# Banded attention and a gated feed-forward: moving the attention steps in the output part, and turning the fourth x tile by DMA

## The chip, the cores and the metric

The kernel runs on one core of a Trainium2 chip. The time is microseconds (us) of device time. Runs of one kernel agree within about half a percent. "Span" is the time from the first to the last instruction in a trace; it is some 2 us shorter than the time of the run. A run counts as fast when it is within 1.5% of the fastest run of its kernel.

## The reference

Attention over 8 batches, 8 heads, 576 tokens, 64 per head, with a band of 32 tokens to either side and 8 global tokens; its result x (4608 tokens by 512) goes through a gated feed-forward.

```python
mask = np.abs(pos[:, None] - pos[None, :]) <= window
mask = mask | is_global[:, None] | is_global[None, :]
scores = np.where(mask, scale * np.matmul(q, k.transpose(0, 1, 3, 2)), -1000000000.0)
attn = softmax(scores)                     # written out in the reference
x = np.matmul(attn, v)                     # then heads side by side: (4608, 512)
ffn_out = gelu(x @ w_gate) * (x @ w_val) @ w_out
out = x + sigmoid(x @ w_res) * ffn_out
```

## The kernel before

Nine chunks of 512 tokens (four tiles of 128). For chunk c an input part makes twelve pairs of products g and v (`g_ps`, `v_ps`), then an output part of 16 steps makes, for each tile t, a gate product (`r_ps`) and three thirds of the output product (`f_ps`). Between these 16 steps stands the attention of chunk c + 1: scores (`sc`), exponentials (`pt`), global rows (`sn`, `vgs`), values (`nd`), the normalised tile (`xtok`), and its turned form (`xt`, its transpose), which the next input part multiplies. A turn is made either by TensorE (four transposes and a copy) or by one DMA, issued on the sync queue. The products are written to banks of PSUM, which the pools `psm` and `pss` hand out; a bank is free again when its reader is done. The reader of a gate product is the tanh on ScalarE, from which the sigmoid is made; the readers of scores are the exponentials. Chunks 1 to 7 have this form; chunk 0 has its own.

```python
psm = ctx.enter_context(tc.tile_pool(name="psm", bufs=4, space=bass.MemoryType.PSUM))
pss = ctx.enter_context(tc.tile_pool(name="pss", bufs=2, space=bass.MemoryType.PSUM))

def scores(c, quad, pps=(0, 1)):
    ...
    for pp in pps:
        pool, tag = (psm, "mm") if pp else (pss, "sc")
        sc = [pool.tile([128, 2, 4, 64], F32, name="sc", tag=tag) for _ in range(2)]
        heads(c, quad, pp, sc, True)
        ...

def turn_x(c, t):
    mine = xt[c % 2][:, :, 128 * t:128 * t + 128]
    if c > 1 and t < 3:
        nc.sync.dma_start(mine, xtok[c % 2][:, t, :], transpose=True)
        return
    tx = pss.tile([128, NKT, 128], BF16, name="tx", tag="sc")
    for kk in range(NKT):
        nc.tensor.transpose(tx[:, kk, :], xtok[c % 2][:, t, 128 * kk:128 * kk + 128], ident)
    (nc.vector.tensor_copy if c or t == 3 else nc.scalar.copy)(mine, tx)

# the end of a tile's third third: the output goes through GpSimd and the sync queue
    nc.vector.scalar_tensor_tensor(prb, held["r"], 1.0, held["f"], ALU.add, ALU.mult)
    nc.gpsimd.tensor_tensor(ob, prb, xtok[c % 2][:, t, :], ALU.add)
    nc.sync.dma_start(out[r0:r0 + 128, :], ob)

# the 16 steps; jobs[n] stand before product n
    jobs[1] += [lambda: half(0), lambda: held_mask[0](0, 4)]
    for t in range(4):
        jobs[5 + 2 * t].append(lambda t=t: values(c + 1, t))
        jobs[7 + 2 * t].insert(0, lambda t=t: turn_x(c + 1, t))
    jobs[4].append(lambda: half(1))
    ...
```

The softmax here doesn't subtract the row's maximum and nothing guards it: scores larger than these inputs give would overflow.

## Time and profile before

The median was 393.49 us of three runs.

| what | before |
|---|---|
| TensorE busy, share of the span | 377.8 us, 97% |
| VectorE, ScalarE, GpSimd | 51%, 43%, 43% |
| share of the last chain on TensorE | 93% |
| output part, chunks 1, 3, 5 | 18.68 us |
| output part, chunks 2, 4, 6 (one tile has two batches) | 18.89 to 18.90 us |
| output part, chunk 7 (no global rows) | 19.06 us |
| first g of chunk 1 (end of the start-up) | 70.35 us |

An output part is measured from the start of its first r product to the start of the next chunk's first g product, both read from TensorE's row.

### The profile page before, as it was taken

How to read it: one execution, taken by the hardware profiler on the slowest of the kernel's cores; microseconds unless marked ns; L12 is line 12 of the kernel's file. 1: busy time of each engine (PE TensorE's matmuls, PEld its weight loads, DVE VectorE, ACT ScalarE, POOL GpSimd, SP SyncE). 2: the span in 40 equal slices, each digit the busy share in tenths (PEclk: the TensorE clock that was granted, in tenths of full speed). 3: DMA queues.
4: the chain of work that ended last, by engine and by line, in shares of the span. 5: the costliest groups of instructions: out<-in, count | busy, mean ns of one | idle time of the engine just before them, and what ended most of it. 6: DMA issues, size and time to landing. Idle time of an engine off the chain costs nothing.

```text
span 391.4 us, 8491 instructions
## 1 busy us (share of the span) xinstructions
PE 377.8 (97%) x3360; PEld 196.8 (50%) x3360; DVE 201.2 (51%) x446; ACT 170.2 (43%) x285; POOL 168.2 (43%) x203
## 2 busy tenths in 40 slices
PE   3989989999999999999999999999999999999996
PEld 2674555444644464445544554455445544554444
DVE  7767684537534664467344643555345533553422
ACT  6753685236243633364335423462337233723321
POOL 7787783958165425562456138612501210121012
PEclk9999999999999999999999999999999999999999
DMA  8999999699659924996399729992990210041002
GB/s 249 258 379 357 239 349 210 129 189 155 105 99 162 169 51 108 133 192 75 106 143 183 79 82 144 199 91 81 118 146 30 72 51 0 2 94 57 0 28 81
DMA packets 153002, 52.78 MB, mean 135 GB/s; under 512 B 136386, under 2 KB 143426, under 8 KB 152962
## 3 DMA queue, kind: packets, MB, share of 16 engines
q1 hardware_dynamic: 77024, 41.88, 44.7%
q0 software_dynamic: 75392, 9.84, 42.9%
q8 instruction: 26, 0.43, 0.5%
q10 hardware_dynamic: 546, 0.52, 0.4%
q14 instruction: 14, 0.11, 0.1%
HBM read 39.19 MB, written 9.44 MB: 124 GB/s over the span
## 4 chain that ended last, share of the span: by engine, by line
PE 93%; DVE 3%; ACT 2%; DMA 1%; issue 1%; SPq 0%; POOL 0%; DVEq 0%; POOLq 0%; ACTq 0%
PE g_ps L630 24%; PE v_ps L630 23%; PE f_ps L686 22%; PE r_ps L656 8%; PE nd L575 5%; PE sc L534 2%; PE nd L587 2%; PE ss L481 1%; PE sg L472 1%; PE tx L610 1%; DMA xt<-xtok 1%; PE sc L523 1%; PE tk L451 1%; PE tq L451 1%; ACT pt L541 1%
## 5 line engine op out<-in xcount | busy, mean ns | idle before, releaser
L639 DVE SCALAR_TENSOR_TENSOR ht<-gsb,v_ps 128x512 bf16<-128x512 bf16 x108 | 74.2, 687 | 97.0 <-PE v_ps L630 91.4
L636 ACT ACTIVATE gsb<-g_ps 128x512 bf16<-128x512 f32 x108 | 64.4, 597 | 124.5 <-PE g_ps L630 124.4
L692 POOL TENSOR_TENSOR ob<-prb,xtok 128x512 f32<-128x512 f32 x35 | 40.2, 1153 | 174.0 <-DVE prb L690 174.0
L630 PE MATMUL g_ps<-xt,wg_t 128*128 128x512 bf16 (+1 forms) x456 | 112.0, 368 | 0.4 <-DMA xt<-xtok 0.4
L630 PE MATMUL v_ps<-xt,wv_t 128*128 128x512 bf16 (+1 forms) x456 | 112.0, 368 | 0.0
L686 PE MATMUL f_ps<-wo_t,ht 128*128 128x512 bf16 x420 | 99.0, 379 | 0.0
L630 PEld LDWEIGHTS <-wg_t 128*128 128x128 bf16 x456 | 43.3, 98 | 49.4 <-issue 0.9
L630 PEld LDWEIGHTS <-wv_t 128*128 128x128 bf16 x456 | 43.4, 98 | 49.1
L686 PEld LDWEIGHTS <-ht 128*128 128x128 bf16 x420 | 40.0, 98 | 39.5
L664 ACT ACTIVATE rsb<-r_ps 128x512 bf16<-128x512 f32 x36 | 21.8, 609 | 67.0 <-PE r_ps L656 67.0
L690 DVE SCALAR_TENSOR_TENSOR prb<-rsb,f_ps 128x512 f32<-128x512 bf16 x35 | 24.0, 686 | 27.2 <-PE f_ps L686 26.3
L656 PE MATMUL r_ps<-wr_t,xt 128*128 128x512 bf16 x144 | 36.9, 380 | 1.1 <-ACT rsb L664 1.0
L541 ACT ACTIVATE pt<-sc 128x512 bf16<-128x512 f32 x64 | 33.2, 620 | 9.5 <-PE sc L534 9.5
L91 POOL DMA_DIRECT2D q_st<-in_q_dram x25 | 21.5, 869 | 19.0 <-DMA qt<-q_st 18.6
L575 PEld LDWEIGHTS <-pt 128*128 128x128 bf16 x576 | 21.9, 97 | 9.3 <-PE r_ps L656 0.7
L557 DVE TENSOR_TENSOR pt<-pt,maskw 128x512 bf16<-128x512 bf16 x56 | 22.4, 421 | 7.1 <-ACT pt L541 5.8
L99 POOL DMA_DIRECT2D ve<-in_v_dram x30 | 25.5, 865 | 0.0
L600 DVE TENSOR_TENSOR xtok<-nd,rden 128x512 bf16<-128x512 f32 x34 | 23.5, 692 | 1.3
L91 POOL DMA_DIRECT2D k_st<-in_k_dram x25 | 21.1, 878 | 4.2 <-DMA kt<-k_st 2.6
L575 PE MATMUL nd<-ve,pt 128*128 128x65 bf16 x320 | 22.4, 193 | 0.6 <-DVE xtok L600 0.6
L599 DVE RECIPROCAL rden<-nd 128x8 f32<-128x8 f32 x34 | 7.0, 207 | 30.3 <-PE nd L587 30.3
L656 PEld LDWEIGHTS <-xt 128*128 128x128 bf16 x144 | 13.0, 97 | 14.8 <-issue 0.9
(174 smaller groups left out, 305.6 us busy)
## 6 DMA issues: line engine op xcount, KB each, us to landing
out_dram<-ob SPq DMA_DIRECT2D x35, 256.0 KB, 2.1
vo<-ve SPq DMA_DIRECT2D x12, 260.0 KB, 5.3
q_st<-in_q_dram POOLq DMA_DIRECT2D x20, 128.0 KB, 5.4
k_st<-in_k_dram POOLq DMA_DIRECT2D x20, 128.0 KB, 6.4
ve<-in_v_dram POOLq DMA_DIRECT2D x18, 128.0 KB, 6.2
wo_t<-in_k_dram SPq DMA_DIRECT2D x8, 256.0 KB, 5.4
vraw<-in_q_dram SPq DMA_DIRECT2D x8, 256.0 KB, 6.8
extra<-in_moe_w_out_dram SPq DMA_DIRECT2D x4, 512.0 KB, 6.7
```

The lines of the kernel that those rows point to most:

```text
L91: nc.gpsimd.dma_start(dst[0:n, r, :].rearrange("p (h d) -> p h d", d=D), src[b].rearrange("h s d -> s h d")[128 * r:128 * r + n])
L99: nc.gpsimd.dma_start(t[p0:p1, c, :, 0:D], v[b].rearrange("h s d -> s h d")[s0 + p0:s0 + p1])
L541: nc.scalar.activation(sc if stay else mine, sc, ACTF.Exp, bias=0.0, scale=SCALE)
L575: nc.tensor.matmul(nds[h // 4][:, VG * (h % 4):VG * (h % 4) + VG], view(pt, 0, 128, c0, [[1, 128]]), vw, start=(h % 4 == 0 and e == 0), st ...
L600: nc.vector.tensor_tensor(xtok[c % 2][:, t, :].rearrange("p (a h d) -> p a h d", a=2, d=D), num[:, :, :, 0:D], view(rden, 0, 128, 0, [[4, ...
L630: nc.tensor.matmul(held[what][:, c0:c1], w[:, kk, 128 * j:128 * j + 128], x[:, kk, c0:c1], start=(kk == 0), stop=(kk == NKT - 1))
L636: nc.scalar.activation(held["s"], held["g"], ACTF.Gelu, bias=0.0, scale=1.0)
L639: nc.vector.scalar_tensor_tensor(ht[:, j, :], held["s"], 0.5, held["v"], ALU.mult, ALU.mult)
L656: nc.tensor.matmul(r_ps, xt[c % 2][:, kk, 128 * t:128 * t + 128], wr_t[:, kk, :], start=(kk == 0), stop=(kk == NKT - 1))
L686: nc.tensor.matmul(held["f"], ht[:, j, 128 * t:128 * t + 128], wo_t[:, j, :], start=(j == 0), stop=(j == NFF - 1))
L690: nc.vector.scalar_tensor_tensor(prb, held["r"], 1.0, held["f"], ALU.add, ALU.mult)
L692: nc.gpsimd.tensor_tensor(ob, prb, xtok[c % 2][:, t, :], ALU.add)
```

## The change

The intent was to take the last TensorE turn out of the output parts and to give the DMA turn that replaces it the time that it needs. The attention steps move about one step earlier: global rows and second scores to step 3, values to steps 4, 6, 8 and 10, each with its turn right behind. The tanh of tile 0 moves behind the first exponentials.

```diff
-        if c > 1 and t < 3:
+        if c > 1:
             nc.sync.dma_start(mine, xtok[c % 2][:, t, :], transpose=True)
...
-        if c == 0:
+        if c == 0 or t == 0:
             gates.append((gate, open_gate))
...
-                jobs[4].append(lambda: global_rows(b))
+                jobs[3].append(lambda: global_rows(b))
...
-            jobs[1] += [lambda: half(0), lambda: held_mask[0](0, 4)]
+            jobs[1] += [lambda: half(0), gates[-1][1], lambda: held_mask[0](0, 4)]
+            jobs[3].append(lambda: half(1))
             for t in range(4):
-                jobs[5 + 2 * t].append(lambda t=t: values(c + 1, t))
-                jobs[7 + 2 * t].insert(0, lambda t=t: turn_x(c + 1, t))
-            jobs[4].append(lambda: half(1))
-            jobs[6].append(lambda: held_mask[1](0, 2))
-            jobs[7].append(lambda: held_mask[1](2, 4))
+                jobs[4 + 2 * t] += [lambda t=t: values(c + 1, t), lambda t=t: turn_x(c + 1, t)]
+            jobs[5].append(lambda: held_mask[1](0, 2))
+            jobs[6].append(lambda: held_mask[1](2, 4))
...
-            work_f[n]()
+            if n == 0 and c + 1 < NCH:
+                gates[-1][0](now=False)
+            else:
+                work_f[n]()
```

## The prediction

> **What bounds the kernel now.** I read the page's busy times first, then the chain of work that ended last, then that chain inside one of the repeated stages, then the waits of every engine there. The kernel handles nine chunks of 512 tokens. Each of chunks 1 to 7 is a feed-forward input part (twelve pairs of g and v products) followed by an output part of 16 steps (per token tile t one gate product r, then three thirds of f), and the attention of the next chunk is woven into those 16 steps. The change touches only these seven output parts.
>
> ```profile
> PE 377.8 (97%) x3360; PEld 196.8 (50%) x3360; DVE 201.2 (51%) x446; ACT 170.2 (43%) x285; POOL 168.2 (43%) x203
> PE   3989989999999999999999999999999999999996
> PEclk9999999999999999999999999999999999999999
> PE 93%; DVE 3%; ACT 2%; DMA 1%; issue 1%; SPq 0%; POOL 0%; DVEq 0%; POOLq 0%; ACTq 0%
> ```
>
> TensorE is busy in nearly every slice from the second to the last but one, at full granted clock, and 93% of the chain that ended last is TensorE. The other engines stand near half. So a microsecond is won only by giving TensorE less to do or by closing a gap in its row. The chain through one output part (chunk 2, attention of chunk 3) shows how few gaps there are. Columns: start in us, length in us, what.
>
> ```profile
> 132.66 0.88 PE r_ps L656 x4
> 133.54 0.57 PE sc L534 x32
> 134.12 2.70 PE f_ps L686 x12
> 136.81 0.17 PE sn L507 x4
> 136.99 0.28 PE sn L510 x20
> 137.27 0.57 PE sc L534 x32
> 137.84 0.97 PE r_ps L656 x4
> ...
> 147.04 0.86 PE f_ps L686 x4
> 147.90 0.86 PE r_ps L656 x4
> 148.77 0.22 PE tx L610 x4
> 148.99 2.59 PE f_ps L686 x12
> 151.58 0.86 PE g_ps L630 x4
> ```
>
> Each row starts where the one before ended: no wait of TensorE in 18.92 us (132.66 to 151.58). Twelve f products take 2.59 us, 0.216 each; four r products 0.86. The only excess is 0.11 us on the f or r row behind each block of scores (2.70, 0.97). The table of waits for TensorE is empty in the output parts of chunks 1 to 6. In chunk 7 it is not:
>
> ```profile
> 353.32 1.02 PE L630 MATMUL g_ps<-xt,wg_t 128*128 128x512 bf16 x4 [0.39 <-DMA xt<-xtok]
> ```
>
> Here the first g product of chunk 8 waited for an x tile turned by DMA. On the sync engine's row the second and third of that chunk's three turns are one merged entry, and the longer part of it is the second alone:
>
> ```profile
> 347.46 4.18 SPq L606 DMA_TRANSPOSE xt<-xtok  x2
> ```
>
> In the earlier chunks the same pair took 2.52 us. So one issue took 2.86 us in place of 1.2, and the third turn came 1.6 us late.
>
> **What the Trainium skill says.** "TensorE: Matmul & The Clock Gate", section "Part 4: PE-mode transpose", gives about 275 ns for a 128x128 transpose in a kernel's context. This trace has 219 ns as the mean of one, but four of them advance the chain by only 0.22 us, because they overlap. The page "Trainium Kernel Development and Optimization", section "Performance Expectations", warns of just this: matmul busy time is a bad metric, since matmuls are pipelined. I use the 0.22. "DMA: Bandwidth & Descriptors", section "Rules for kernel authors", advises to issue a DMA early and wait for its semaphore late, so that the fixed cost overlaps; the trace agrees, as the x turns take a median of 2.4 us from issue to landing and six of seven chunks never wait for one. "Runtime: NRT & Kernel Launch", section "Instruction fetch mechanics", says that each engine fetches its program through its own DMA queue in blocks of 16 KiB. The page lists 26 such packets of 0.43 MB together, one of them in the 8 us around the slow issue above; that it caused the slowness is a guess.
>
> **The change, part by part.** The built program's order confirms what the diff says.
>
> Removed: in seven chunks the TensorE turn of tile 3 (four transposes with their weight loads, 28 in all) and its VectorE copy (425 ns, seven of them). Read from the table of groups, 28 x 219 ns would be 6.1 us; read from the chain it is 7 x 0.22 = 1.55 us. The copy lies on a half-idle engine: nothing.
>
> Added: seven DMA turns on the sync queue, about 1.2 us of issue each and 2.4 to 2.7 us to landing. This queue is idle for most of the output part.
>
> Moved on TensorE: the products themselves are the same. A block of scores is followed by f in both places now, so the two excesses of 0.11 us stay. The tile chains: values at steps 4, 6, 8, 10 in place of 5, 7, 9, 11. Between values 1, 2 and 3 still stand 1.73 us of products (two f thirds, or one f third and one gate), which the normalisation on VectorE must fit into: from the end of values 1 to the end of its masks took 1.64 us in chunk 2 (142.17 to 143.81). It fits by 0.09 us, as before, and the masked half that comes last is read some 0.24 us later.
>
> The new last turn: values 3 end at X. The normalised tile is ready at about X + 0.97 (147.04 to 148.01 before). The third turn is issued by about X + 0.6, so the fourth starts at X + 1.0 and lands at X + 3.4 to 3.7. The next g product comes at X + 1.73 (two f thirds) + 0.86 (gate) + 2.59 (three thirds) = X + 5.18. Slack 1.4 us or more. Hidden, in the rule.
>
> The gate of tile 0: its tanh now stands behind the first four exponentials. Exponentials start 0.45 us behind their scores and follow at 0.49 us. With r at 0, scores start at 0.88, exponentials run 1.33 to 3.3, tanh ends near 3.9. The next scores take the PSUM bank of that gate in their second half, at 0.88 + 0.57 + 1.84 (eight f) + 0.45 (sn) + 0.29 = 4.03. It fits by about 0.1 us. In chunk 7 there are no global rows (no sn), so the same point comes at 3.58 and TensorE waits some 0.35 us. Against that, in the kernel before, a similar wait in chunk 7 cost about 0.1 us.
>
> The end of chunk 7: before, g starts 0.55 us later than the sequence of products alone would have it (353.32 against 352.77). With tiles 0 to 2 issued earlier and the fourth with 1.4 us of slack I expect this to go.
>
> Sum: 6 x 0.22 = 1.33; chunk 7: 0.22 + 0.55 + 0.1 - 0.35 = 0.52. Together 1.85 us. I keep back 0.15 for the two fits of 0.1 us. 393.49 - 1.7 = 391.8.
>
> **Rivals.** First: the fourth DMA turn becomes the wait. If one issue is slow by 1.6 us (as at 347.46) and it is the third or fourth turn of a chunk, landing comes at X + 5.0 to 5.3, against X + 5.0 for the first weight load of g: up to 0.3 us per case, more if landing is slow too. The program of TensorE is shorter by 8 instructions a chunk, so block fetches fall elsewhere. Even one such case in each of seven chunks is some 2 us, which makes the time 393.6. For it speaks the chunk 7 wait; against it that five of six other chunks show no issue over 1.25 us and none shows a wait. Second: ScalarE's late tanh or the masks hold the second scores or values 2 in every chunk. Each fit is 0.1 us; were I wrong by 0.3 us in both, 7 x 0.4 = 2.8 us of loss would give about 394.5. Against it: both relations are worked out from the same trace's pitches, and the masks' relation is unchanged. Third: the moved work closes hidden bubbles, and more than the turns is won. Speaking against it: the chain has no gap in chunks 1 to 6, so beyond 2 us there is nothing to win in these stages; 391.0 at best.
>
> **Range and chances.** The three runs of before spread over 1.1 us, so a median may be off by half a microsecond. With the rivals, 390.9 to 393.4 should hold it 8 times in 10. The 2% limit is 7.9 us away: faster by 2% would need more than five times the removed work, slower by 2% over 1.3 us of new wait in every chunk. Within 2%: 0.98; faster 0.01; slower 0.01.
>
> **What will show it.** Right, if the chain through chunk 2's output part has no transposes and lasts about 18.7 us, if TensorE's waits stay empty in chunks 1 to 6, if the first g product of chunk 8 has no DMA wait any more, and if the scores of chunk 7 wait 0.3 to 0.4 us for the tanh. Wrong, if g products show waits for x tiles in several chunks, if the second scores wait for the tanh in chunks 1 to 6, or if the time per chunk fell by clearly more than 0.22 us.

## The result, and the profile after

The changed kernel took 391.89 us (median of six, 391.42 to 392.42) against 393.51. The ratio is 0.995, with a 95% interval of 0.9929 to 0.9971: within 2%, as forecast. A ratio here is the mean time of one kernel's fast runs over that of the other's of the same rounds, so it is not quite the ratio of the medians.

The page of the changed kernel shows the same picture as before, a little shorter:

```profile
PE 372.5 (96%) x3281; PEld 195.5 (50%) x3332; DVE 200.7 (52%) x439; ACT 171.6 (44%) x285; POOL 169.0 (43%) x203
PE   3989989999999999999999999999999999999996
```

TensorE still bounds it. Its busy time cannot be compared with before to a microsecond, because the trace holds 3281 of its products and 3332 of their weight loads: some records of products are missing. Positions in time are safe. The second trace of the changed kernel holds all 3332 of both: TensorE is busy for 376.3 us there, 1.5 us less than before.

The chain through the output part of chunk 2 in the changed kernel (start, length, what):

```profile
134.61 1.83 PE f_ps L686 x8
136.45 0.17 PE sn L507 x4
...
146.45 0.22 PE nd L587 x2
146.68 0.05 issue
146.73 1.67 PE f_ps L686 x7
148.40 0.86 PE r_ps L656 x4
149.27 2.59 PE f_ps L686 x12
151.86 0.86 PE g_ps L630 x4
```

The `tx` row is gone, and g follows f at once. The small "issue" row stands where a record is missing (seven f products are listed of eight): rows still start where those before them end. The output part lasts 18.68 us in place of 18.90.

| output part of chunk | 1 | 2 | 3 | 4 | 5 | 6 | 7 |
|---|---|---|---|---|---|---|---|
| before, us | 18.68 | 18.90 | 18.68 | 18.89 | 18.68 | 18.90 | 19.06 |
| after, us | 18.45 | 18.68 | 18.46 | 18.67 | 18.46 | 18.67 | 18.01 |

Six chunks gain 1.34 us together and chunk 7 gains 1.05: 2.39 us. The spans differ by only 1.7 us (391.4 and 389.7), because the changed kernel came to chunk 1 later in this trace, at 71.07 us in place of 70.35. Input parts and the tail after the first g of chunk 8 are alike to 0.04 us.

Chunk 7 is where the reading was too coarse. This is the chain of the kernel before at the head of that output part:

```profile
335.33 0.60 ACT rsb L664
335.93 0.02 issue
335.94 1.28 ACT L541
337.23 0.01 issue
337.24 2.07 ACT pt L541 x4
339.31 0.04 issue
339.35 1.02 PE r_ps L656 x4
```

The tanh stands first, then the load of the exponential table (1.28 us), then four exponentials, and only their end releases the second gate product. In the changed kernel the table load comes ahead of the tanh, while TensorE still works on the gate, and the same place is on TensorE throughout:

```profile
334.67 0.57 PE sc L534 x32
...
337.08 0.57 PE sc L534 x32
337.65 0.97 PE f_ps L686 x4
```

### The profile page after: what moved, and what is told of

Same layout as the page of the kernel before. It is cut to its first block, busy times and chain, and to the rows that moved or that the text cites. A ratio compares the mean times of both kernels' runs of the same rounds, so it can differ in the third digit from the quotient of the medians.

```text
span 389.7 us, 8394 instructions
## 1 busy us (share of the span) xinstructions
PE 372.5 (96%) x3281; PEld 195.5 (50%) x3332; DVE 200.7 (52%) x439; ACT 171.6 (44%) x285; POOL 169.0 (43%) x203
## 4 chain that ended last, share of the span: by engine, by line
PE 90%; DVE 3%; DMA 2%; issue 1%; ACT 1%; POOL 1%; SPq 0%; DVEq 0%; POOLq 0%
PE g_ps L630 24%; PE v_ps L630 23%; PE f_ps L686 22%; PE r_ps L656 7%; PE nd L575 4%; PE sc L534 3%; PE nd L587 2%; DMA extra<-in_k_dram 2%; PE ss L481 1%; PE sg L472 1%; DVE pt L557 1%; PE sc L523 1%; PE tk L451 1%; PE tq L451 1%; PE sn L510 1%
## 5 line engine op out<-in xcount | busy, mean ns | idle before, releaser
L686 PE MATMUL f_ps<-wo_t,ht 128*128 128x512 bf16 x398 | 96.7, 379 | 1.8 <-issue 1.0
L656 PE MATMUL r_ps<-wr_t,xt 128*128 128x512 bf16 x134 | 35.6, 378 | 1.3 <-ACT rsb L664 0.9
L557 DVE TENSOR_TENSOR pt<-pt,maskw 128x512 bf16<-128x512 bf16 x56 | 24.7, 461 | 4.1 <-ACT pt L541 2.8
L575 PE MATMUL nd<-vo,pt 128*128 128x65 bf16 x256 | 19.7, 193 | 0.4 <-PE r_ps L656 0.3
```

The source lines that it names most:

```text
L557: nc.vector.tensor_tensor(m, x, view(maskw, 0, 128, 64 * i0, [[0, 2], [64, 4], [1, 64]]), ALU.mult)
L575: nc.tensor.matmul(nds[h // 4][:, VG * (h % 4):VG * (h % 4) + VG], view(pt, 0, 128, c0, [[1, 128]]), vw, start=(h % 4 == 0 and e == 0), st ...
L656: nc.tensor.matmul(r_ps, xt[c % 2][:, kk, 128 * t:128 * t + 128], wr_t[:, kk, :], start=(kk == 0), stop=(kk == NKT - 1))
L686: nc.tensor.matmul(held["f"], ht[:, j, 128 * t:128 * t + 128], wo_t[:, j, :], start=(j == 0), stop=(j == NFF - 1))
```

## The experiments

Nine kernels ran, all with correct results. Seven were timed in rounds beside the kernel before.

### The changed kernel again

No edit.

> The changed kernel again, with five rounds. Theory A: the output parts lose 2.4 us in all (six times 0.22 and 1.06 in chunk 7, as in the first profiles), and the 0.72 us by which the changed kernel reached chunk 1 later in its first profile (71.07 against 70.35) is the spread of the start-up, which the change does not touch; then the median should be 1.6 to 2.4 us below before (ratio 0.994 to 0.996), and the first g of chunk 1 in this profile may fall anywhere from 70 to 71.5. Rival B: the later start-up belongs to the change; then the first g of chunk 1 is again near 71.1 and the ratio stays at 0.9957 or above.

Measured: 391.10 us against 393.66, ratio 0.9941 (0.9927 to 0.9954). The output parts were the same to 0.01 us, 18.01 in chunk 7 again. The first g of chunk 1 stood at 70.76 us. Over the traces with an unchanged start-up (these two, the kernel before twice, and the experiments on the output parts below) it moved between 70.35 and 71.59 us, with the kernel before at 70.35 and 71.06. The later start belongs to the spread of the start-up and not to the change. Rival B falls.

### The kernel before again

No edit, a single look.

> The kernel before again, for one more look at the start-up and at which DMA turn is issued slowly. Theory A: the first g of chunk 1 moves by some tenths of a microsecond from 70.35, output parts of chunks 1 to 6 last 18.68 and 18.90 us again. Chunk 7 loses about 0.3 us to the exponentials in every run (that is in the order of the program), while the 0.55 us at its end appear only if a block of program is fetched during the second or third turn again.

Measured: 393.44 us, span 391.7. The output parts were as before but for two. Chunk 5 took 18.88 in place of 18.68. The list of waits names nothing, but the semaphore events in the trace do: of the sixteen parts in which the third turn reports its landing, fifteen were in by 272.13 us and the last came at 273.74, while a 16 KiB block of program had been fetched from 271.57 to 272.55. The weight load of the next g had to wait for it (0.50 us idle, 0.12 in the first trace), and g began 0.20 us late:

```profile
273.84 0.56 PEld L630 LDWEIGHTS <-wg_t 128*128 128x128 bf16 x4 [0.50 <-issue]
```

So a turn can also land late although it was issued in the usual 1.2 us. Chunk 7 took 18.54 us in place of 19.06, and no wait is listed before its first g, although its second turn was issued slowly again (2.18 us). So of the 0.83 us that chunk 7 lost in the first trace, some 0.3 belong to the order of the program and 0.5 to the chance that a slow issue is slow enough.

### The fourth turn by DMA, in the old order

```diff
 # the kernel before
-        if c > 1 and t < 3:
+        if c > 1:
```

> The old order of steps with tile 3 turned by DMA too, nothing else. Theory A: in the old order the fourth turn stands on the sync queue behind the output of tile 2, whose data are ready only about 2.9 us after values 3 end; issued there, it lands about 1.5 us after the next chunk's first g could start, so each of seven chunks gains 0.22 and loses about 1.6: 9 to 10 us slower than before, near 403 us (ratio 1.02 to 1.03). The first g of chunks 2 to 8 shows a wait for the x tile. Rival: a DMA turn is hidden wherever it stands; then 7 x 0.22 faster than before, near 392 us.

Measured: 405.03 us, ratio 1.0286 (1.027 to 1.0302), that is 11.4 us slower. All seven first g products waited for the turned tile, 11.8 us in all. TensorE's row at the end of chunk 2's output part:

```profile
151.51 2.75 PE L686 MATMUL f_ps<-wo_t,ht 128*128 128x512 bf16 x12
155.88 1.02 PE L630 MATMUL g_ps<-xt,wg_t 128*128 128x512 bf16 x4 [1.62 <-DMA xt<-xtok]
```

And the sync queue's, where the fourth turn stands behind the output of tile 2:

```profile
152.89 0.34 SPq L694 DMA_DIRECT2D out_dram<-ob  x1
153.33 1.22 SPq L606 DMA_TRANSPOSE xt<-xtok  x1
```

Values 3 had ended at 149.94, so the tile was ready about 1 us later; the turn stood 2.4 us in the queue behind an output that it has nothing to do with, and landed at 155.74. The turn alone is a loss of 2.9%. The loss was a little larger than the 9 to 10 us expected: 1.56 us in chunk 2 where 1.4 had been worked out.

### The order alone

```diff
 # the changed kernel
-        if c > 1:
+        if c > 1 and t < 3:
...
-                jobs[4 + 2 * t] += [lambda t=t: values(c + 1, t), lambda t=t: turn_x(c + 1, t)]
+                jobs[4 + 2 * t].append(lambda t=t: values(c + 1, t))
+                jobs[4 + 2 * t if t < 3 else 13].append(lambda t=t: turn_x(c + 1, t))
```

> The new order of steps with tile 3 still turned by TensorE, between its gate and its first third, as before. Theory A: in chunks 1 to 6 the order alone is worth nothing (the output part lasts 18.68 us without and 18.90 us with two batches in one tile, as before); in chunk 7 the 0.83 us of waits go. So 0.8 us faster than before, 1.5 us slower than the changed kernel, near 392.7 us. Rival: the order is the main gain and the DMA turn worth little; then the output parts of chunks 1 to 6 last near 18.45 and 18.67 us as in the changed kernel.

Measured: 393.37 us against 393.66, ratio 0.9992 (0.9979 to 1.0006). The output parts of chunks 1 to 6 were 18.68 and 18.89 or 18.90 us, as before; chunk 7 took 18.23. So the order by itself wins nothing in six chunks, and in chunk 7 it wins what the two waits had cost. The 0.22 us from 18.23 to the 18.01 of the changed kernel are the four transposes. The time alone, 0.3 us faster with an interval of about 0.5 us to either side, could not have told this: the 0.8 us that had been expected lie at the edge of that interval.

### The tanh first

```diff
 # the changed kernel
-            jobs[1] += [lambda: half(0), gates[-1][1], lambda: held_mask[0](0, 4)]
+            jobs[1] += [lambda: half(0), lambda: held_mask[0](0, 4)]
...
-                gates[-1][0](now=False)
+                gates[-1][0]()
```

> The changed kernel with the tanh of tile 0 issued at once, ahead of the first exponentials, as in the kernel before. Theory A: chunks 1 to 6 do not change (exponentials about 0.2 us later, nobody waits for them). In chunk 7 the tanh stands ahead of the load of the exponential table, which can then start only some 2.3 us later; the second scores, which come one third of f earlier than in the kernel before, need the banks of the first: TensorE waits about 1.1 us there. Total 1.1 us slower than the changed kernel, all of it in the output part of chunk 7 (19.1 against 18.0 us). Rival C: the place of the tanh matters nowhere; same time as the changed kernel and 18.0 us in chunk 7. Rival D, as my prediction had it: a tanh behind the exponentials holds up the second scores; then this kernel is faster than the changed one in chunk 7 or equal.

Measured: 392.14 us, 1.04 us slower than the changed kernel of the same call (391.10). Chunk 7 took 18.99 us in place of 18.01; chunks 1 to 6 stayed at 18.45 and 18.67 or 18.68, but for 18.53 in chunk 5. TensorE's row in chunk 7:

```profile
337.35 0.19 PE L534 MATMUL sc<-qt,kt 64*128 64x64 bf16 x1 [0.19 <-ACT pt L541]
337.83 0.88 PE L534 MATMUL sc<-qt,kt 64*128 64x64 bf16 x31 [0.30 <-ACT pt L541]
```

The second scores wait for exponentials, whose banks they need, and these came late because the table load stood behind the tanh. So the place of the tanh matters in one chunk of seven, by 1 us, and in the direction opposite to my prediction: behind the exponentials is the better place. Rivals C and D fall.

### The fourth turn behind the output of tile 2

```diff
 # the changed kernel
-                jobs[4 + 2 * t] += [lambda t=t: values(c + 1, t), lambda t=t: turn_x(c + 1, t)]
+                jobs[4 + 2 * t].append(lambda t=t: values(c + 1, t))
+                jobs[4 + 2 * t if t < 3 else 12].append(lambda t=t: turn_x(c + 1, t))
```

> The changed kernel with only the fourth DMA turn moved behind the output of tile 2 on the sync queue. Theory A: that output is issued about 4.0 us after values 3 end (150.49 against 146.5 in chunk 2 of the changed kernel); the turn follows 0.4 us later and lands 2.4 to 2.7 us after that, 1.6 to 2.0 us later than the next g could start. Seven chunks: 11 to 14 us slower than the changed kernel, 403 to 406 us. Rival: the sync queue's order does not matter because the turn is hidden either way; same as the changed kernel, 392 us.

Measured: 404.09 us, ratio 1.0254 to before (1.0223 to 1.0284), some 12 us slower than the changed kernel by the ratios (0.9941 and 0.995). The chain at the end of chunk 2's output part now runs over the turn:

```profile
151.21 1.66 PE f_ps L686 x8
152.87 2.42 DMA xt<-xtok
155.29 0.14 issue
155.43 1.02 PE g_ps L630 x4
```

The turn itself takes the usual 2.42 us. Only its place in the queue differs from the changed kernel, whose sync row is this:

```profile
145.62 0.35 SPq L694 DMA_DIRECT2D out_dram<-ob  x1
146.07 2.83 SPq L606 DMA_TRANSPOSE xt<-xtok  x2
150.49 0.34 SPq L694 DMA_DIRECT2D out_dram<-ob  x1
```

There the third and fourth turns go out as a pair ahead of the output of tile 2. Together with the turn in the old order this settles what the new order is for.

### The program of TensorE shifted

```diff
 # the changed kernel, ahead of the first product of the program
+    spare = psm.tile([128, 64], F32, name="spare", tag="mm")
+    for n in range(64):
+        nc.tensor.matmul(spare, sel[0:NG, :], sel[0:NG, 0:64], start=True, stop=True)
```

> The changed kernel with 64 small spare products of TensorE (128 instructions with their weight loads) at the very start, where TensorE has little to do; their result is not used. Half a block of program shifts where its blocks are fetched. Theory F: a DMA turn of x is issued slowly (over 1.3 us) only when a 16 KiB block of program is fetched during its issue. Then the third turn in chunk 4 and the first in chunk 6, slow in the changed kernel's profile (2.67 and 2.36 us), are back at 1.2 us, and any slow ones are others, among those at which fetches should now fall: one each in chunks 1, 2, 4, 5, 6 and 7. Rival: slow issues belong to the place or to other DMA traffic; then the same turns are slow again. The output parts stay at 18.45 and 18.67 us, unless a slow fourth turn makes one g wait some tenths. The start-up may be up to 1.5 us longer.

Measured: 393.54 us in a single look, with the first g of chunk 1 at 73.22 us, some 2.3 us later, more than the 1.5 I allowed. The output parts were those of the changed kernel to 0.01 us. The slow issues moved. In the changed kernel's trace chunk 4 has its slow turn in the second pair (third turn, 2.67 us):

```profile
221.58 2.81 SPq L606 DMA_TRANSPOSE xt<-xtok  x2
226.47 3.98 SPq L606 DMA_TRANSPOSE xt<-xtok  x2
```

With the program shifted it is in the first pair (first turn, 2.47 us):

```profile
223.73 3.77 SPq L609 DMA_TRANSPOSE xt<-xtok  x2
228.62 3.04 SPq L609 DMA_TRANSPOSE xt<-xtok  x2
```

The first turn of chunk 6 also went back to 1.2 us. Slow ones were the third turn of chunk 2, the first of chunk 4, the fourth of chunk 6 and the second of chunk 7; of the six chunks in which I had put a fetch beside a turn, four had a slow turn and two had none, so the theory does not quite say when. Each of the four had a 16 KiB fetch under way during its issue. Over all traces here but those of the two attempts on chunk 1 below, every x turn over 1.3 us had one, 25 turns; eleven with a fetch beside them were issued in 1.2 us all the same. In the attempts on chunk 1, three turns of chunk 1 itself took 1.32 to 1.44 us without one. That no slow issue in these output parts came without a fetch, and that shifting the program moves the slowness, is shown; how a fetch holds the issue up is not.

The landing is touched as well. Of the 231 x turns in the same nine traces, 39 landed more than 3.0 us after the start of their issue, in place of 2.4, and each had a fetch under way between issue and landing; without one, none took longer than 2.9. None of these slow turns cost TensorE anything in the new order, where g comes about 1.5 us after the usual landing (151.69 against 150.14 in chunk 2); the closest was the slow third turn of chunk 4, after which the fourth landed at 231.71 and g came at 232.31. But no fourth turn was itself late by the 1.6 us of chunk 5 above. If one is, some 0.2 us should be lost (an estimate: the third turn of that chunk landed at the same distance from g).

### Chunk 1 too, first attempt

```diff
 # the changed kernel
-        if c > 1:
+        if c > 0:
             nc.sync.dma_start(mine, xtok[c % 2][:, t, :], transpose=True)
```

> An attempt to beat both: the four tiles of chunk 1 turned by DMA as well, in the same places of the program. It removes 16 more TensorE transposes (0.22 us for four in the chain, 0.9 us in all) and four VectorE copies. Theory A, if the turns stay hidden: 0.9 us faster than the changed kernel. Rival: the sync queue there first issues ten loads of raw q and k, and transfers under that load took 5 to 7 us to land in place of 2.4; then the first g of chunk 1 waits for the last turn, 1 to 3 us, and the kernel is no faster or is slower than the changed one.

Measured: 400.48 us, ratio 1.0161 (1.0136 to 1.0186): slower than both, and by more than the rival had said. The first g of chunk 1 came at 78.96 us. The sync queue shows why:

```profile
64.81 6.88 SPq L199 DMA_DIRECT2D vraw<-in_q_dram  x5
71.80 5.90 SPq L606 DMA_TRANSPOSE xt<-xtok  x4
```

and TensorE's row what it cost:

```profile
78.96 1.89 PE L630 MATMUL g_ps<-xt,wg_t 128*128 128x512 bf16 x4 [8.77 <-DMA xt<-xtok]
```

Four turns stood behind ten loads that themselves waited for GpSimd to free their place. After a gap of 8.8 us TensorE also ran at about half its pace at first (1.89 us for four products in place of 1.02 in the row of the turn alone; the granted clock was 0.50 from 78.9 to 83 us), so the input part of chunk 1 took 24.32 us in place of 21.80.

### Chunk 1 too, second attempt

```diff
 # on top of the first attempt
-            for what in "kq":
-                load_second(what)
+            load_second("k")
...
-            cast_second("q", 0, 1, POOL)
...
             turn_x(1, 3)
+            load_second("q")
...
-            cast_second("q", 1, NQT, POOL)
+            cast_second("q", 0, NQT, POOL)
```

> A second attempt at chunk 1: its four tiles turned by DMA, and the five loads of raw q for batch 2 moved behind them on the sync queue (with GpSimd's cast of the first of them moved to the end). In the first attempt the last turn was issued at 74.95 us, because these q loads stood in front and themselves waited for GpSimd. Theory A: the turns are now issued from about 63 to 67.5 us and land by 70, so the first g of chunk 1 comes at about its old time or up to 0.9 us earlier; but the q loads, the k turns and the q turns of batch 2 shift 3 to 5 us later, and the global scores at the end of chunk 1's input part, which came with 3 to 5 us to spare, may wait up to 3 us. So 1 us faster to 2 us slower than the changed kernel. Rival: the q loads have room; 0.9 us faster than the changed kernel, the best of all.

Measured: 394.65 us, ratio 1.0023 to before (0.9985 to 1.0061), so slower than the changed kernel, by some 3 us if the ratios are compared, which is more than the 2 us that I allowed. The first g of chunk 1 stood at 72.12 us, outside the spread of the others, and its input part took 22.87 us in place of 21.80, with the chain running over the late q loads and the gathers behind them. The 0.9 us of transposes are not to be had this way. No version here beats the changed kernel.

## Why the prediction was right

The time was right to 0.1 us, 391.89 against 391.8, but part of that is luck: two errors in chunk 7 and the spread of the start-up met.

- The removed turn was sized right: 0.22 us a chunk from the chain. Six chunks gave 1.34 us where 1.33 had been worked out. The 219 ns that each transpose lasts in the table of groups would have promised four times as much.
- The last turn was placed right. Values 3 end at X = 146.68 us in chunk 2; the fourth turn was issued at 147.71 (X + 1.03), takes 2.4 us, and g comes at X + 5.18. No first g waited, in this trace or in any other with the fourth turn in this place, from chunk 2 on. What the prediction did not say is that the old order would have lost 11.4 us with the same turn.
- "In chunk 7 ... TensorE waits some 0.35 us" failed. The step was "the next scores take the PSUM bank of that gate in their second half". The times had been worked out well: the tanh ended 3.95 us after the start of r, where 3.9 had been said. But the second scores started into their second half at 337.25 us, after the third and fourth exponentials (336.62 and 337.11) and before the tanh had ended (337.60), so that bank was not the gate's. In the kernel before, only the third exponential holds that half up (338.81, and it starts at 338.86) and the second gate product waits for the fourth, so there one of the two banks seems to have been the gate's. It seems that banks are handed on in the order in which they are released, so that moving the tanh changed which bank came next; this was not tested by itself. The measured wait was nil.
- "A similar wait in chunk 7 cost about 0.1 us" was sized too small. It was about 0.3 us (18.54 without a wait at its end, against 18.23 with the order alone).
- The 0.55 us at the end of chunk 7 did go, but they were there only in some runs: 0.5 in the first trace, nothing in the second.
- The sum should thus read 1.34 + 0.22 + 0.3 + 0 to 0.5, which is 1.9 to 2.4 us. The two sets of rounds measured 1.6 us (393.51 to 391.89) and 2.6 us (393.66 to 391.10), and their intervals hold both ends.
- The first rival, that a slow issue makes g wait, was right about slow issues and wrong about their cost: up to 2.67 us was hidden. A slow third turn delays the fourth by less than it loses, because it starts before values 3 end (226.47 us against about 227.3 in chunk 4). That no fourth turn was slow or late by 1.6 us in these traces is luck, though it would cost tenths only. The second, late masks or tanh, showed in no chunk. The third, hidden bubbles, was half right in chunk 7 alone.

## What to carry to other kernels

When TensorE is full, price a removed piece of its work by what it advances the chain, not by the duration of its records, and check on stages that repeat to 0.01 us when whole runs vary by more than the effect. A DMA that replaces such work is free only if its queue lets it go: here the same turn went with a gain of 0.5% or a loss of 2.5 to 2.9% by whether one unrelated output stood in front of it in an in-order queue. Moving a small instruction on another engine may also change which buffer the next user gets, so read the waits of the built program before counting on a buffer.

## What the Trainium skill lacked or had wrong

- "DMA: Bandwidth & Descriptors" gives sequencer cycles of a DMA turn only for small tiles out of HBM and for one very large case, and no time to landing. Here a 128x512 bf16 turn takes 1.2 us of issue and 2.4 us to landing, and the next entry of the sync queue waits for the issue.
- "Runtime: NRT & Kernel Launch", "Instruction fetch mechanics", calls the cost of crossing a 16 KiB block mostly hidden. On TensorE's own row this held: with its program shifted by half a block the output parts stayed the same to 0.01 us. But a DMA turn on the sync queue issued during such a fetch took up to 2.9 us in place of 1.2, turns landed up to 2 us late, and shifting the program moved the slow turns. One late landing cost TensorE 0.20 us (kernel before, chunk 5).
- "TensorE: Matmul & The Clock Gate", "Back-to-back issue gap", gives about 131 ns per product of 512 columns as the sustained pace beside weight loads. Here twelve take 2.59 us, 216 ns each, throughout, which the section gives for an isolated product only; the section "Wait — 56ns, not 53.3ns?" of the same page has 215.7 ns for products in a row.
- "ScalarE: Activation LUTs", "What ACT_TABLE_LOAD costs", adds a drain of about 1380 ns to the load's 1283. The load lasted 1.28 us here, but it started at 335.94, as the tanh before it ended, and the first exponential followed at 337.24: no drain is to be seen.
